# Second chunk's keys and state in 120 rows, state products per unit of eight heads

## The chip, the core and the metric

The kernel runs on one core of a Trainium2 chip. The core has a matrix engine (TensorE, PE in the profile, with its weight loads as PEld), a vector engine (VectorE, DVE), a scalar engine (ScalarE, ACT), GpSimd (POOL), and SyncE (SP), whose queue issues all of this kernel's transfers. They run side by side and wait for each other by semaphores. The metric is the time of the program on the device, in microseconds; lower is better. PE's clock is granted at 2.4 GHz (1.00 in the profile) or at half of it (0.50).

## What is computed

An mLSTM attention of 4 batches, 8 heads, 768 steps and 40 columns a head, and behind it two feed-forward layers over its 3072 rows of 320 columns, with 2048 hidden columns each:

```python
def _attn_ref(q, k, v, i_gate, f_gate, o_gate):
    ...
    for t in range(S):
        m_new = np.maximum(f_gate[:, :, t] + m, i_gate[:, :, t])
        f_stab = np.exp(f_gate[:, :, t] + m - m_new)
        i_stab = np.exp(i_gate[:, :, t] - m_new)
        ...
        C = f_stab[...] * C + i_stab[...] * np.einsum('bhd,bhe->bhde', vt, kt)
        n = f_stab[...] * n + i_stab[...] * kt
        h_tilde = np.einsum('bhde,bhe->bhd', C, qt)
        denom = np.maximum(np.abs(nq), 1.0)
        y[:, :, t] = o * h_tilde / denom

r = np.maximum(x @ w_in, 0.0);  x = (r * r) @ w_out
h = x @ w_in2;  x = np.where(h > 0, h, np.exp(np.minimum(h, 0)) - 1) @ w_out2
```

## The kernel before

**Tiling.** The steps are cut into 6 chunks of 128. A unit `u` is one chunk of one batch (24 units, 4 to a chunk), a half unit `n = 2u + g` is four of its heads. The state of a batch, 40 rows by 8 heads of 42 columns (values, the normalizer, a zero), is kept in `Cf[b]` across chunks.

**One half unit.** `mb_load` brings rows of running maxima, `mask` (POOL) and `emit_E` (ACT) make decay weights of them, `scores` (L283) multiplies keys and queries on PE into the bank `s`, `emit_P` (DVE, L289) joins both. `pv` (L302) then issues three kinds of products: `inter`, queries by state (`pv<-cf,rqk`, later `pv<-cst,qks`), `main`, weights by values (`pv<-kvo,mb`), and `st`, keys by values (`ut<-kvo`), which the state takes up. `evac` (DVE) joins the first two into `num` (L329, L333) and updates the state: a decay (L332) and an addition (L335). `norm`, `trans`, `x_hi` and `x_lo` finish a unit and lay it out as input of the first layer.

**Chunks differ.** The first chunk (`m_pe` to `evac0`) is written by hand and runs in the order of the code. In the second chunk (half units 8 to 15, below `NPLAIN`) queries, keys and state are plain 32-bit numbers in 40 rows (`qk_load`, `qk_hi`), and each product is two matmul instructions. From the third chunk on they are split in parts and stacked in 120 rows (`qk_stack`, `Cst`), with one instruction each. A form such as 40\*128 in the profile is the rows by the columns of the weights that an instruction uses.

**What sets the order.** Attention for the tile of 512 rows that comes next is woven into the feed-forward steps of the first layer. Steps of attention (`attn_pre`, `attn_pe`, `attn_post`, two to a half unit) are dealt out over the 16 hidden blocks of a tile; `emit_pe` puts their matmuls between the large ones `h<-xh,w` (first product) and `acc<-ghi,w` (second). During the first tile the weights are brought in as well (`raw<-wq`), and DVE and ACT convert them (`ct`, `cu`, `w`). Up to attention step 16 the order of PE, ACT, DVE and POOL is that of the code; behind it a scheduler sets the order of every engine at build time, and SP's throughout. PSUM banks `s`, `pv` and `ut` exist once each; `ut` also serves the transposes.

Of the kernel before, what the change touches and what calls it, by code (L numbers as in the profile page):

```python
# [6 lines left out]
F32 = mybir.dt.float32  # L7
# [34 lines left out]
def body(tc, qk, kvo, gates, wq, ident_in, qkm_in, out):  # L42
# [102 lines left out]
    Cf = [gc.tile([D, H * VW], F32, name=f"cf{b}") for b in range(B)]  # L145
# [80 lines left out]
    def qk_load(n):  # L226
        if n < N0:
            t = wp.tile([128, 2 * WC], F32, tag="w", name="rqk")[0:3 * D, 0:8 * L].rearrange("p (two t) -> p two t", two=2)
        else:
            t = a2.tile([3 * D, 2, 4 * L], F32, tag="qks" if n < NPLAIN and n % 2 else "rqk", name="rqk")  # L230
        k_ = D if n < NPLAIN else 3 * D
        sp.dma_start(out=t[0:k_], in_=qk[n, 0:k_])
        raw_t[n] = t

    def qk_hi(n):
        if n < NPLAIN:
            t = raw_t.pop(n)
            qS[n], kS[n] = t[0:D, 0], t[0:D, 1]
            return
        st = a2.tile([3 * D, 2, 4 * L], F32R, tag="qks", name="qks")  # L240
        act.activation(out=st, in_=raw_t[n], func=AF.Copy)
        qS[n], kS[n] = st[:, 0], st[:, 1]
# [48 lines left out]
    def pv(n):  # L291
        u, g = divmod(n, 2)
        c, b = divmod(u, B)
        p = mb_t.pop(n)
        q_ = qS.pop(n)
        t = kvo_t[u]
        ps = bank(n, "pv")
        PV_t[n] = ps
        inter, main, st = [], [], []

        def mm(to, o, l_, r_):
            to.append(lambda: pe.matmul(o, lhsT=l_, rhs=r_, start=True, stop=True))  # L302
# [12 lines left out]
        return inter, main, st

    def evac(n):
# [7 lines left out]
        cf3 = Cf[b][:, 4 * g * VW:4 * (g + 1) * VW].rearrange("p (h d) -> p h d", h=4)  # L325
        if keyed(u):
            u3 = U_t.pop(n)[0:D, 0:4 * VW].rearrange("p (h d) -> p h d", h=4)
        gb = cols[c % 2][:, 64 + b * H + 4 * g:64 + b * H + 4 * g + 4].unsqueeze(2).to_broadcast([128, 4, VW])
        dve.tensor_tensor(out=nu, in0=p[:, 4 * VW:8 * VW].rearrange("p (h d) -> p h d", h=4), in1=gb, op=ALU.mult)  # L329
        if keyed(u):  # L330
            db = decb[c % 2][:, b * H + 4 * g:b * H + 4 * g + 4].unsqueeze(2).to_broadcast([D, 4, VW])
            dve.tensor_tensor(out=cf3, in0=cf3, in1=db, op=ALU.mult)  # L332
        dve.tensor_tensor(out=nu, in0=pm, in1=nu, op=ALU.add)  # L333
        if keyed(u):
            dve.tensor_tensor(out=cf3, in0=u3, in1=cf3, op=ALU.add)  # L335
# [293 lines left out]
    def evac0(n):  # L629
# [5 lines left out]
        act.activation(out=Cf[u][:, 4 * g * VW:4 * (g + 1) * VW], in_=ps[0:D, 4 * VW:8 * VW], func=AF.Copy)  # L635
# [14 lines left out]
    pool_.affine_select(out=negmask, in_=mz, pattern=[[0, 4], [1, L]], compare_op=ALU.is_ge, fill=NEG, base=0, channel_multiplier=-1)  # L650
    early = es.enter_context(ExitStack())
# [134 lines left out]
def _layout(inputs):  # L786
# [12 lines left out]
    qk = np.concatenate([qk] * 3, axis=1)  # L799
    qkm = np.zeros((3 * D, 2), np.float32)  # L800
# [42 lines left out]
```

## Time and profile before

| | |
|---|---|
| three timed runs | 905.93, 900.64, 907.98 us (median 905.93) |
| profiled execution | 900.38 us, span 898.6 us, mean clock 0.978 |
| PE busy | 880.1 us, 98% |
| DVE busy | 556.1 us, 62% |
| ACT busy | 548.8 us, 61% |
| POOL busy | 140.3 us, 16% |
| transfers | 81.82 MB, mean 91 GB/s |

The profile is of one execution on the chip. Busy shares are means over stages with different limits, so the rows below are mostly of short stretches. Matmuls are pipelined, so an instruction's length overlaps the next one's; what a group of matmuls takes is read from its start to the start of the next group.

### The profile page before, as it was taken

The numbers are of one execution on the slowest core, as the hardware profiler recorded it, in microseconds if no ns is written. First come the engines' busy times: TensorE is split into PE (matmuls) and PEld (weight loads), VectorE is DVE, ScalarE is ACT, GpSimd is POOL, SyncE is SP. The second block draws the span as 40 slices with busy tenths as digits, with TensorE's granted clock in tenths as the row PEclk, the third lists the DMA queues.
The fourth block names the chain that finished last, engine by engine and source line by source line (L and its number), as shares of the span: only waits on it lengthen the run. The fifth ranks groups of instructions, "written<-read, shape, count | busy, mean of one in ns | idle before, by whom it ended". The sixth has DMA issues, their size and how long they took to land.

```text
span 898.6 us, 13340 instructions
## 1 busy us (share of the span) xinstructions
PE 880.1 (98%) x4813; PEld 744.0 (83%) x4818; DVE 556.1 (62%) x1027; ACT 548.8 (61%) x1045; POOL 140.3 (16%) x203
## 2 busy tenths in 40 slices
PE   9889999999999999999999998999999999999997
PEld 5768778778888887888888887898989999899996
DVE  2668978755555554454543699766566656655654
ACT  3549867555666566666746799555464555554543
POOL 1142013221211111110000000211112111111111
PEclk9867999999999999999999999999999999999999
DMA  8525453753343445334204354001020020000000
GB/s 248 194 96 162 163 177 116 208 99 83 111 131 95 105 121 151 100 102 142 80 25 158 108 196 144 1 28 50 1 77 1 1 77 1 22 9 1 30 1 30
DMA packets 31875, 81.82 MB, mean 91 GB/s; under 512 B 4578, under 2 KB 9666, under 8 KB 31810
## 3 DMA queue, kind: packets, MB, share of 16 engines
q1 hardware_dynamic: 31809, 80.98, 30.3%
q8 instruction: 38, 0.62, 0.3%
q14 instruction: 28, 0.22, 0.1%
HBM read 70.51 MB, written 8.73 MB: 88 GB/s over the span
## 4 chain that ended last, share of the span: by engine, by line
PE 85%; DMA 6%; DVE 4%; ACT 3%; issue 1%; POOL 0%; SPq 0%; POOLq 0%; DVEq 0%; ACTq 0%
PE h L485 38%; PE acc L526 36%; PE pv L302 5%; PE s L283 2%; DMA mb<-negm_dr 2%; PE ut L302 1%; DMA kvo<-kvo 1%; DMA rqk<-qk 1%; PE ut L376 1%; DMA yr<-y_dr 1%; PE pv L622 1%; DVE w L137 1%; DMA dec_dr<-gaw 1%; ACT mb L275 0%; DMA decb<-dec_dr 0%
## 5 line engine op out<-in xcount | busy, mean ns | idle before, releaser
L485 PE MATMUL h<-xh,w 128*128 128x512 f32 x1152 | 369.1, 405 | 3.2 <-DVE r L507 3.0
L485 PEld LDWEIGHTS h<-xh,w 128*128 128x128 f32 x1152 | 219.0, 191 | 48.4 <-DVE r L507 3.8
L509 DVE TENSOR_TENSOR glo<-r,ghi 128x512 fp32r<-128x512 f32 x192 | 132.2, 689 | 155.7 <-ACT r L499 85.1
L485 PE MATMUL h<-xl,w 128*128 128x512 f32 x384 | 155.0, 404 | 1.4 <-DVE xl L393 1.3
L526 PE MATMUL acc<-w,ghi 128*128 128x320 f32 x768 | 153.6, 309 | 0.6 <-POOL ghi L508 0.6
L503 ACT ACTIVATE r<-h 128x512 f32<-128x512 f32 x96 | 57.4, 598 | 144.1 <-PE h L485 98.5
L526 PE MATMUL acc<-ghi,w 128*128 128x512 f32 x480 | 139.8, 403 | 0.0
L526 PEld LDWEIGHTS acc<-w,ghi 128*128 128x128 f32 x768 | 126.0, 188 | 6.6 <-POOL ghi L508 1.1
L508 POOL TENSOR_SCALAR ghi<-r 128x512 fp32r<-128x512 f32 x96 | 61.3, 638 | 358.2 <-DVE r L507 137.9
L506 DVE SCALAR_TENSOR_TENSOR ex<-ex,th 128x512 f32<-128x512 f32 x96 | 68.5, 713 | 57.2 <-ACT ex L505 56.0
L526 PEld LDWEIGHTS acc<-ghi,w 128*128 128x128 f32 x480 | 88.0, 189 | 16.0
L526 PE MATMUL acc<-w,glo 128*128 128x320 f32 x384 | 99.2, 309 | 0.0
L275 ACT ACTIVATE mb<-mb,cols 128x128 f32<-128x128 f32 x160 | 51.4, 390 | 71.0 <-POOL mb L267 71.0
L526 PE MATMUL acc<-glo,w 128*128 128x512 f32 x288 | 89.8, 404 | 1.7 <-DVE glo L509 1.7
L485 PEld LDWEIGHTS h<-xl,w 128*128 128x128 f32 x384 | 73.8, 192 | 14.7 <-DVE xl L393 2.0
L497 ACT ACTIVATE r<-h 128x512 f32<-128x512 f32 x96 | 55.6, 585 | 35.1 <-PE h L485 31.7
L507 DVE SCALAR_TENSOR_TENSOR r<-h,ex 128x512 f32<-128x512 f32 x96 | 66.2, 690 | 2.8
L526 PEld LDWEIGHTS acc<-w,glo 128*128 128x128 f32 x384 | 67.4, 188 | 0.2
L498 ACT ACTIVATE ghi<-r 128x512 fp32r<-128x512 f32 x96 | 60.3, 628 | 10.2 <-PE acc L526 8.4
L267 POOL TENSOR_SCALAR_AFFINE_SELECT mb<-mb 128x512 f32<-128x512 f32 x40 | 33.1, 830 | 189.1 <-DMA mb<-negm_dr 138.1
L504 ACT ACTIVATE th<-r 128x512 f32<-128x512 f32 x96 | 60.7, 632 | 2.8
L526 PEld LDWEIGHTS acc<-glo,w 128*128 128x128 f32 x288 | 51.7, 188 | 11.8 <-DVE glo L509 2.3
(96 smaller groups left out, 1051.4 us busy)
## 6 DMA issues: line engine op xcount, KB each, us to landing
raw<-wq SPq DMA_DIRECT2D x32, 704.0 KB
rqk<-qk SPq DMA_DIRECT2D x32, 480.0 KB
kvo<-kvo SPq DMA_DIRECT2D x24, 488.0 KB
mb<-negm_dr SPq DMA_DIRECT2D x40, 256.0 KB
y_dr<-y SPq DMA_DIRECT2D x18, 256.0 KB
out<-y SPq DMA_DIRECT2D x24, 160.0 KB
yr<-y_dr SPq DMA_DIRECT2D x12, 256.0 KB
yr<-y_dr SPq DMA_DIRECT2D x24, 128.0 KB
```

Of the source, the lines that this page charges most:

```text
L275: act.activation(out=m[:, i, :], in_=m[:, i, :], func=AF.Exp, bias=cols[c % 2][:, col:col + 1])
L302: to.append(lambda: pe.matmul(o, lhsT=l_, rhs=r_, start=True, stop=True))
L485: lambda i=i, a=a, b_=b_: pe.matmul(h[:, 0:n], lhsT=a, rhs=b_, start=(i == 0), stop=(i == len(seq) - 1))
L497: act.activation(out=r, in_=h, func=AF.Relu)
L498: act.activation(out=hi, in_=r, func=AF.Square)
L503: act.activation(out=r, in_=h, func=AF.Relu, scale=-1.0)
L504: act.activation(out=th, in_=r, func=AF.Tanh, scale=0.5)
L506: dve.scalar_tensor_tensor(out=ex, in0=ex, scalar=1.0, in1=th, op0=ALU.add, op1=ALU.mult)
L507: dve.scalar_tensor_tensor(out=r, in0=h, scalar=0.0, in1=ex, op0=ALU.max, op1=ALU.subtract)
L508: pool_.tensor_scalar(out=hi, in0=r, scalar1=1.0, scalar2=1.0, op0=ALU.mult, op1=ALU.mult)
L509: dve.tensor_tensor(out=lo, in0=r, in1=hi.bitcast(F32), op=ALU.subtract)
L526: ops.append(lambda: pe.matmul(o, lhsT=l_, rhs=r_, start=first and st, stop=last and sp_))
```

## The change

- `qk_load` fetches 120 rows, not 40, for half units 8 to 15. The host fills the query rows 40 to 119 with copies and the key rows 40 to 119 with zeros.
- `Cf` has 120 rows, which four POOL memsets clear at the start; only rows 0 to 39 are written later. The products of the second chunk then run over 120 rows, and what the added rows contribute is zero.
- `pv` issues no state products for the first half of a unit (`g` = 0) and those of all 8 heads with the second, into one bank. `evac` decays and updates the state of all 8 heads at once, behind the second half; the two operations on `num` now stand before the state's.

```diff
-    Cf = [gc.tile([D, H * VW], F32, name=f"cf{b}") for b in range(B)]
+    Cf = [gc.tile([3 * D, H * VW], F32, name=f"cf{b}") for b in range(B)]
...
-        k_ = D if n < NPLAIN else 3 * D
+        k_ = D if n < N0 else 3 * D
         sp.dma_start(out=t[0:k_], in_=qk[n, 0:k_])
...
-            qS[n], kS[n] = t[0:D, 0], t[0:D, 1]
+            qS[n], kS[n] = t[:, 0], t[:, 1]
...
-        if keyed(u):
-            ut = bank(n, "ut")
-            U_t[n] = ut
         for i in range(4):
...
             mm(main, ps[:, o], p[:, i, :], v1)
-            if keyed(u):
-                mm(st, ut[0:D, o], t[:, h * D:(h + 1) * D], v1)
+        if keyed(u) and g:
+            U_t[u] = bank(n, "ut")
+            for h in range(H):
+                mm(st, U_t[u][0:D, h * VW:(h + 1) * VW], t[:, h * D:(h + 1) * D], t[:, DM + h * VW:DM + (h + 1) * VW])
...
-        if keyed(u):
-            db = decb[c % 2][:, b * H + 4 * g:b * H + 4 * g + 4].unsqueeze(2).to_broadcast([D, 4, VW])
+        dve.tensor_tensor(out=nu, in0=pm, in1=nu, op=ALU.add)
+        if keyed(u) and g:
+            cf3 = Cf[b][0:D].rearrange("p (h d) -> p h d", h=H)
+            u3 = U_t.pop(u)[0:D, 0:H * VW].rearrange("p (h d) -> p h d", h=H)
+            db = decb[c % 2][:, b * H:b * H + H].unsqueeze(2).to_broadcast([D, H, VW])
             dve.tensor_tensor(out=cf3, in0=cf3, in1=db, op=ALU.mult)
-        dve.tensor_tensor(out=nu, in0=pm, in1=nu, op=ALU.add)
-        if keyed(u):
             dve.tensor_tensor(out=cf3, in0=u3, in1=cf3, op=ALU.add)
...
+    for x in Cf:
+        pool_.memset(x, 0.0)
...
+    qk[:NPLAIN, D:, 1] = 0.0
```

The scheduler makes a new order from the first changed instruction on. On PE, where the second chunk begins, the order before is as follows (`ut<-kvo` state products, `s` scores, `pv<-cf` queries by state, `pv<-kvo,mb` weights by values, `h` feed-forward; a row with x4 is four products):

```order
L302 MATMUL ut<-kvo 40x42 x4
L283 MATMUL s<-rqk 128x128 x4
L302 MATMUL pv<-kvo,mb 128x42 x4
L302 MATMUL ut<-kvo 40x42 x4
L283 MATMUL s<-rqk 128x128 x4
L302 MATMUL pv<-cf_126,rqk 128x42 x4
L302 MATMUL pv<-kvo,mb 128x42 x4
L283 MATMUL s<-rqk 128x128 x4
L485 MATMUL h<-xh,w 128x512
```

And in the changed kernel, at the same place on PE:

```order
L302 MATMUL ut<-kvo 40x42 x8
L283 MATMUL s<-rqk 128x128 x4
L302 MATMUL pv<-kvo,mb 128x42 x4
L283 MATMUL s<-rqk 128x128 x4
L482 MATMUL h<-xh,w 128x512
L482 MATMUL h<-xl,w 128x512
L482 MATMUL h<-xh,w 128x512 x2
L482 MATMUL h<-xl,w 128x512
L482 MATMUL h<-xh,w 128x512 x3
L302 MATMUL pv<-cf_126,rqk 128x42 x4
L302 MATMUL pv<-kvo,mb 128x42 x4
```

The second group of state products has moved up to the first, and eight large matmuls now stand between the scores and the queries by state.

On DVE, from the second chunk's first decay on (`cf` the state, `num` the numerator, `mb` the joined scores, `ct` and `w` the conversion of a weight tile), before:

```order
L332 TENSOR_TENSOR cf_126<-cf_126,decb_121 40x168
L289 TENSOR_TENSOR mb<-s,mb 128x512
L335 TENSOR_TENSOR cf_126<-ut,cf_126 40x168
L289 TENSOR_TENSOR mb<-s,mb 128x512
L329 TENSOR_TENSOR num<-pv,cols_119 128x168
L333 TENSOR_TENSOR num<-pv,num 128x168
L137 TENSOR_TENSOR w<-ct,w 128x64
L137 TENSOR_TENSOR w<-ct,w 128x640
L289 TENSOR_TENSOR mb<-s,mb 128x512
L332 TENSOR_TENSOR cf_126<-cf_126,decb_121 40x168
L119 TENSOR_SCALAR ct<-ct 128x704
L335 TENSOR_TENSOR cf_126<-ut,cf_126 40x168
```

In the changed kernel, on DVE at that place:

```order
L289 TENSOR_TENSOR mb<-s,mb 128x512 x2
L325 TENSOR_TENSOR num<-pv,cols_119 128x168
L326 TENSOR_TENSOR num<-pv,num 128x168
L289 TENSOR_TENSOR mb<-s,mb 128x512
L137 TENSOR_TENSOR w<-ct,w 128x64
L137 TENSOR_TENSOR w<-ct,w 128x640
L119 TENSOR_SCALAR ct<-ct 128x704
L331 TENSOR_TENSOR cf_126<-cf_126,decb_121 40x336
L120 SCALAR_TENSOR_TENSOR ct<-raw,ct 128x704
L332 TENSOR_TENSOR cf_126<-ut,cf_126 40x336
```

The four state operations of the unit have become two of twice the columns, behind the third score product.

On SP, where the third chunk's gates are stored (`negm_dr`, `dec_dr`) and fetched again (`mb` mask rows, `decb` decays), with weight loads `raw`, before:

```order
L96 DMA raw<-wq 128x704
L180 DMA negm_dr<-gnm 32x128
L184 DMA dec_dr<-gaw 32x1
L356 DMA cst_123<-cst_123 40x336
L357 DMA cst_123<-clo 40x336
L223 DMA mb<-negm_dr 128x512
L187 DMA decb_120<-dec_dr 40x32
```

And in the changed kernel, on SP:

```order
L96 DMA raw<-wq 128x704
L180 DMA negm_dr<-gnm 32x128
L232 DMA rqk<-qk 120x1024
L184 DMA dec_dr<-gaw 32x1
L96 DMA raw<-wq 128x704
L223 DMA mb<-negm_dr 128x512 x2
L187 DMA decb_120<-dec_dr 40x32
```

A weight load has moved in between the store of the decays and the mask rows, and the state's two transfers `cst` have moved ahead of this place.

## Rows read from the trace of the kernel before

**Rows 1.** The page: busy time, share of the span, instructions; the clock in 40 slices

```profile
PE 880.1 (98%) x4813; PEld 744.0 (83%) x4818; DVE 556.1 (62%) x1027; ACT 548.8 (61%) x1045; POOL 140.3 (16%) x203
...
PEclk9867999999999999999999999999999999999999
```

**Rows 2.** Windows: length, busy us (instructions) of PE, PEld, DVE, ACT, POOL; PEclk, DMA share, GB/s

```profile
62.97:69.79 6.82, 5.48 (x14) 4.20 (x14) 6.28 (x10) 5.72 (x17) 4.39 (x5) 0.50 0.58 195
...
73.20:76.62 3.42, 3.42 (x32) 3.27 (x30) 3.29 (x10) 3.42 (x10) 0.25 (x1) 1.00 0.40 92
76.62:83.45 6.83, 6.83 (x26) 5.10 (x26) 6.79 (x14) 6.83 (x16) 3.15 (x4) 0.50 0.50 168
...
114.17:117.58 3.41, 3.41 (x22) 2.67 (x23) 3.25 (x8) 1.78 (x3) 0.00 (x0) 1.00 0.03 10
117.58:120.99 3.41, 3.41 (x11) 2.73 (x11) 0.62 (x2) 0.00 (x0) 0.44 (x1) 0.50 0.43 152
...
165.37:168.78 3.41, 2.94 (x29) 2.49 (x28) 2.79 (x8) 2.83 (x8) 1.44 (x2) 1.00 0.83 234
...
175.61:895.80 720.19, 712.54 (x3893) 616.41 (x3891) 429.91 (x753) 439.09 (x815) 102.20 (x161) 1.00 0.25 72
```

**Rows 3.** Timeline of PE, second chunk: start, length, line, operands, form, instructions

```profile
71.85 1.09 PE L302 MATMUL pv<-kvo,mb 128*128 128x42 f32 x8
72.87 0.50 PE L302 MATMUL ut<-kvo 128*40 128x42 f32 x8
...
74.30 0.98 PE L302 MATMUL pv<-cf,rqk 40*128 40x42 f32 x8
75.21 1.09 PE L302 MATMUL pv<-kvo,mb 128*128 128x42 f32 x8
76.22 1.74 PE L283 MATMUL s<-rqk 40*128 40x128 f32 x8
...
115.77 1.08 PE L302 MATMUL pv<-cf,rqk 40*128 40x42 f32 x8
116.78 1.23 PE L302 MATMUL pv<-kvo,mb 128*128 128x42 f32 x8
```

**Rows 4.** Timeline of PE, third chunk

```profile
166.90 1.07 PE L302 MATMUL pv<-kvo,mb 128*128 128x42 f32 x8
167.79 0.52 PE L376 MATMUL ut<-ident,xt 128*128 128x128 f32 x3
```

**Rows 5.** Windows: VectorE alone, from 63 to 118 us

```profile
63.00:118.00 55.00, 48.96 (x96) 0.87 0.46 152
```

**Rows 6.** Groups of VectorE by form: instructions, busy us, mean ns, idle before them

```profile
L367 DVE TENSOR_TENSOR num<-num,den 128x320 f32<-128x320 f32 x24 | 13.4, 559 | 0.6
...
L332 DVE TENSOR_TENSOR cf<-cf,decb 40x168 f32<-40x168 f32 x32 | 10.3, 354 | 28.5 <-DMA decb<-dec_dr 14.4 <-POOL clo L350 12.7 <-PE pv L302 1.3
L335 DVE TENSOR_TENSOR cf<-ut,cf 40x168 f32<-40x168 f32 x32 | 10.2, 319 | 2.5 <-PE ut L302 2.4
```

**Rows 7.** Windows of the start, columns as in rows 2

```profile
4.00:26.00 22.00, 21.68 (x140) 14.58 (x139) 6.57 (x20) 8.27 (x26) 1.40 (x2) 1.00 0.95 290
...
32.00:38.00 6.00, 5.84 (x48) 4.79 (x48) 5.32 (x12) 5.15 (x14) 1.85 (x2) 1.00 0.12 25
```

**Rows 8.** Timeline of POOL at the start

```profile
1.19 0.52 POOL L649 MEMSET mz<- 128x512 f32 x1
...
11.28 1.40 POOL L263 TENSOR_TENSOR kvo<-kvo,cols 128x320 f32<-128x320 f32 x2 [8.85 <-DVE cols L196]
```

**Rows 9.** Groups of weight loads by form, columns as in rows 6

```profile
L302 PEld LDWEIGHTS pv<-kvo,mb 128*128 128x128 f32 x320 | 47.5, 191 | 4.2
...
L302 PEld LDWEIGHTS pv<-cf,rqk 40*128 40x128 f32 x64 | 8.1, 187 | 3.3 <-issue 2.5 <-PE acc L526 0.7
```

**Rows 10.** Waits of the DMA queue up to 130 us: us in total, times, longest

```profile
SPq L96 <- DVE ct L120: 37.5, 10, 7.3
```

**Rows 11.** Timeline of VectorE where the third chunk's decay begins

```profile
121.52 1.30 DVE L332 TENSOR_TENSOR cf<-cf,decb 40x168 f32<-40x168 f32 x5 [3.32 <-DMA decb<-dec_dr]
```

More of the change, by code (lines that the diff above doesn't have):

```diff
@@ L324, in evac @@
         pm = p[:, 0:4 * VW].rearrange("p (h d) -> p h d", h=4)
-        cf3 = Cf[b][:, 4 * g * VW:4 * (g + 1) * VW].rearrange("p (h d) -> p h d", h=4)
-        if keyed(u):
-            u3 = U_t.pop(n)[0:D, 0:4 * VW].rearrange("p (h d) -> p h d", h=4)
         gb = cols[c % 2][:, 64 + b * H + 4 * g:64 + b * H + 4 * g + 4].unsqueeze(2).to_broadcast([128, 4, VW])
         dve.tensor_tensor(out=nu, in0=p[:, 4 * VW:8 * VW].rearrange("p (h d) -> p h d", h=4), in1=gb, op=ALU.mult)
-        if keyed(u):
-            db = decb[c % 2][:, b * H + 4 * g:b * H + 4 * g + 4].unsqueeze(2).to_broadcast([D, 4, VW])
+        dve.tensor_tensor(out=nu, in0=pm, in1=nu, op=ALU.add)
[3 more added lines that the diff above has]
+            db = decb[c % 2][:, b * H:b * H + H].unsqueeze(2).to_broadcast([D, H, VW])
             dve.tensor_tensor(out=cf3, in0=cf3, in1=db, op=ALU.mult)
-        dve.tensor_tensor(out=nu, in0=pm, in1=nu, op=ALU.add)
-        if keyed(u):
             dve.tensor_tensor(out=cf3, in0=u3, in1=cf3, op=ALU.add)
@@ L343, in c_hi @@
             b = u % B
-            act.activation(out=Cst[b][0:D], in_=Cf[b], func=AF.Copy)
+            act.activation(out=Cst[b][0:D], in_=Cf[b][0:D], func=AF.Copy)
     def c_lo(u):
@@ L349, in c_lo @@
             clo = a1.tile([D, H * VW], F32R, tag="clo", name="clo")
-            pool_.tensor_tensor(out=clo, in0=Cf[b], in1=Cst[b][0:D].bitcast(F32), op=ALU.subtract)
+            pool_.tensor_tensor(out=clo, in0=Cf[b][0:D], in1=Cst[b][0:D].bitcast(F32), op=ALU.subtract)
             clo_t[u] = clo
@@ L634, in evac0 @@
         dve.tensor_copy(num_t[u][:, 4 * g:4 * g + 4, :], ps[:, 0:4 * VW].rearrange("p (h d) -> p h d", h=4))
-        act.activation(out=Cf[u][:, 4 * g * VW:4 * (g + 1) * VW], in_=ps[0:D, 4 * VW:8 * VW], func=AF.Copy)
+        act.activation(out=Cf[u][0:D, 4 * g * VW:4 * (g + 1) * VW], in_=ps[0:D, 4 * VW:8 * VW], func=AF.Copy)
     dr = gc.tile([128, TT], BF16, name="dr")
```

## Prediction

> **What bounds the kernel now.** I read the page first: TensorE (PE) is busy for 98% of the span, and the clock row shows dips in the first quarter only [rows 1]. So the time is the sum of PE's own work, at the clock it is granted, and what shortens that work is worth its full length as long as no other engine steps in.
>
> Next I cut the early part into stretches where the clock stands still [rows 2]. The second chunk, the one the change touches, runs from about 60 us on. In it PE stands at 0.50 (1.2 GHz) three times: 62.97 to 69.79, 76.62 to 83.45 and 117.58 to 120.99, 17.06 us in all. Before the second fall there is no gap at all: PE is busy 3.42 of 3.42 us, with key-query products `s<-rqk` and state products `pv<-cf,rqk` in the form 40\*128, beside `pv<-kvo,mb` [rows 2, 3]. Before the third it is busy 3.41 of 3.41 us, again with `pv<-cf,rqk` and `pv<-kvo,mb` [rows 2, 3]. A stretch of like small matmuls in the third chunk, where the operands have 120 rows (165.37 to 168.78), ran at 1.00 and was not followed by a fall at once, though PE was busy for only 2.94 of 3.41 us [rows 2, 4].
>
> Third, I looked at what it costs PE to go from one array shape to another. The eight instructions `pv<-kvo,mb` take 0.89 us to the start of the next group where that group has the full 128\*128 shape (166.90 to 167.79, [rows 4]), and 1.02 and 1.01 us where the next is 128\*40 or 40\*128 (71.85 to 72.87, 75.21 to 76.22, [rows 3]). One change of shape costs about 0.12 us.
>
> Last, VectorE (DVE) in this stage: from 63 to 118 us it works 48.96 of 55.00 us [rows 5]. It converts the weights here, so it is nearly a second bound.
>
> **The change, part by part.** *40 rows become 120.* The matmuls stay as many and stream as many columns. Eight `pv<-cf,rqk` of 40 rows take 1.01 us to the next group, with a change of shape at the end (115.77 to 116.78); eight of 128 rows take 0.89 without one [rows 3, 4]. Less the 0.12 they are alike, so more rows cost nothing. What goes is the change of shape around them. Through the whole order of PE after the hand-ordered start, I count 139 changes of shape before and 69 after. About 52 of the 70 that go lie in the second chunk's stage: all those into and out of the 40-row form, and a few of the state product's. At 0.12 each that is 6.2 us; if only the way out is paid for, since a small group in the full shape may also wait on its way in, 3.1.
>
> *The state product per unit.* Two groups of eight 128\*40 instructions become one of sixteen, where the scheduler leaves them together. Of the 70 changes, about 18 fall into chunks three to five: 18 x 0.12 = 2.2 us, bounds 1.1 and 2.2. PE is alone in its way there (712.54 busy of 720.19 us, [rows 2]), so I take it in full.
>
> *The clock.* If the second chunk's stretches look to the clock like the third chunk's, the three dips go. Their price is half of PE's busy time in them: (5.48 + 6.83 + 3.41)/2 = 7.9 us [rows 2]. The lower bound is zero.
>
> *What DVE lets through.* So PE could give back up to 6.2 + 7.9 = 14.1 us between 60 and 121 us. DVE has 55.00 - 48.96 = 6.0 us free there [rows 5], and its order is fixed, so PE's products wait for it once that is used up. Its own work shrinks: per unit two decays of 354 ns and two additions of 319 ns become one each over 336 columns [rows 6]. No row has 40x336. The bounds are the 168-column time and twice that; nearest is the 128x320 multiplication at 559 ns, which holds some slow ones, so I take 530 ns. A unit then saves 2 x (354 + 319) - 2 x 530 = 286 ns, the four units of this stage 1.1 us. The stage can thus shrink by about 7.1 us. Not every idle gap of DVE closes, because its waits are for particular products; I take three quarters, 5.5 us. Bounds: 1.1 (DVE's own saving alone) and 7.1.
>
> *Loads.* Eight query-key loads grow from 160 to 480 KB, 2.6 MB in all. At 290 GB/s [rows 7] each takes 1.1 us longer. Four are issued in the first 26 us, where the DMA engines are at 0.95; the 4.4 us they add run into the quiet stretch from 32 to 38 us (share 0.12, [rows 7]), and nothing due before it is queued behind them but the second chunk's gates, mask rows and keys, which are used from 60 us on. The other four come singly between 62 and 105 us. Cost zero; without this cover 1.1 us each.
>
> *Clearing the state.* Four POOL memsets of 120x336, no more than 0.52 us each by the 128x512 one, at most 2.1 us. POOL is idle for 8.85 us before it is next wanted at 11.28 [rows 8], and the mask's first reader on PE stands behind the same gate columns. Cost zero; 2.1 us if POOL were waited for.
>
> Here a rule speaks against the change. The loads of weights take 187 ns in the 40\*128 form and 191 ns in the full one [rows 9], and both kinds of group advance by 0.11 us per matmul [rows 3, 4], so loads lie under other matmuls in either form. The Trainium skill (TensorE: Matmul & The Clock Gate, Part 3, "The mechanism") says that a weight load overlaps matmuls in flight only when the row group differs. With 120 rows all row groups are taken, so by that rule loads would no longer be hidden; by the rows they are hidden already in the full shape. By the rows nothing is added; the rule's sum is the third rival below.
>
> **Sum.** 5.5 + 2.2 = 7.7 us off the profiled run's 900.4 (a span of 898.6 and 1.8 us around it): 892.7. The profiled run sits at the low end: the timed runs are 900.6, 905.9 and 908.0, a median 5.5 us above it. One trace cannot show what the higher two did. Falls of the clock that come without any gap are the likeliest thing to differ from run to run, and the change removes these; I carry 2 us of the 5.5. Forecast: 894.5 us.
>
> **Rivals.** (a) *The added rows are zeros and earn no clock.* For it: nothing in this trace separates rows addressed from rows that hold data. Against it: first-chunk work aside, the dips follow the 40-row form. Then the dips stay, the shape changes give about the mean of 3.1 and 6.2, 4.6, plus 2.2, within DVE's room; the spread of the runs stays too: 905.9 - 6.8 = 899.1.
>
> (b) *DVE is the bound of the stage.* For it: 89% busy while it is also held up by PE. Then the stage gives DVE's own 1.1 and the late part 2.2: 900.4 - 3.3 = 897.1, and with half of the runs' spread 900.
>
> (c) *Weight loads come into the open.* 128 matmul instructions of the second chunk at 0.19 us each add 24.3 us to the forecast: 919. It decides from 0.16 us per matmul on: 128 x 0.16 = 20.5 us take 894.5 to 915. Against it stand the equal group times above.
>
> (d) *The SyncE queue.* In the new order a weight load `raw` stands ahead of two mask loads and of `decb`. Such a load has stood up to 7.3 us for DVE [rows 10], and DVE's decay of the state already waited 3.32 us for `decb` [rows 11], and a score product stands behind that decay in both orders. If the raw load waits 7.3 us there, mask rows and `decb` come that much later, PE starves for it, and a half-clock stretch like the third (3.41 us busy, 1.7 lost, [rows 2]) follows: 9.0 - 7.7 = +1.3, 907. It makes the kernel slower by over 1% only from a hold of about 15 us. For it: the order. Against: it is one load, and the 37.5 us that ten such loads stood before are 3.8 us each in the mean.
>
> **How the numbers follow.** Forecast (891 to 897) 0.50; (a) 0.20; (b) 0.16; (c) 0.02; (d) 0.08, of which 0.03 for a long hold; and 0.04 for a larger gain than DVE's room suggests, about 886. What a measurement of this kernel tells from no change is about 1%, so under 896.9 counts as faster and over 915.0 as slower. Forecast and larger gain make 0.54; a little of the forecast lies above 896.9 and a little of (a) below, which cancel. Slower: 0.02 + 0.03 = 0.05. Same: 0.41. The range 885 to 906 leaves out (c) and most of (d), and the far tail below. The forecast's own range is 889 to 898.
>
> **What would show it.** Right: granted clock 1.00 between 62 and 121 us but for stretches behind a real gap; `pv<-cf,rqk` and `s<-rqk` as 120\*128, eight `pv<-kvo,mb` in 0.89 us everywhere; DVE's state updates near 530 ns, its idle time from 63 to 118 us below 3 us; span near 891. Wrong: dips behind 120-row stretches without a gap (a); PE idle on `glo`, `xl` or `mb` of DVE in that stage (b); a group's spacing above 0.11 us at full clock (c); PE idle behind mask loads with SyncE standing on `ct` (d).

## Result: 898.55 us, 0.8% under the kernel before

The changed kernel takes 898.55 us (median of 8 runs, 893.61 to 899.45); the kernel before, timed beside it, 905.32 us (8 runs, 899.85 to 907.98). The ratio is 0.9917 with a 95% interval of 0.9893 to 0.9942: a gain clear of noise, but less than the 1% below which I had counted a time as "same" (over 896.9 us). I had given "faster" 0.54 and "same" 0.41. The value lies inside the range 885 to 906, 4.05 us above the forecast of 894.5 and 0.6 above the forecast's own range of 889 to 898. Ratios, here and further down, leave out runs over 1.5% above their kernel's fastest (five of e7's twelve, one each of e8's and e11's six); medians and ranges leave out none.

The profiled run of the changed kernel took 898.73 us (span 896.9). Its page, the lines that answer to [rows 1]:

```profile
PE 873.7 (97%) x4818; PEld 744.5 (83%) x4818; DVE 554.8 (62%) x995; ACT 549.0 (61%) x1045; POOL 138.7 (15%) x207
...
PEclk9669998999999999999999999999999999999999
```

TensorE works 6.4 us less, and its low clock has moved: it now stands at the very start of the row. The windows of the same trace, cut where the clock changes (columns as in [rows 2]):

```profile
30.59:61.31 30.72, 30.05 (x142) 24.20 (x143) 14.84 (x34) 10.90 (x29) 3.55 (x4) 0.50 0.50 159
61.31:136.41 75.10, 68.63 (x418) 55.95 (x416) 64.33 (x129) 61.24 (x122) 16.96 (x18) 1.00 0.54 173
136.41:143.23 6.82, 6.82 (x20) 5.76 (x21) 6.27 (x13) 5.46 (x9) 2.56 (x2) 0.50 0.90 250
143.23:894.16 750.93, 739.48 (x4072) 640.57 (x4070) 457.92 (x789) 460.19 (x854) 109.11 (x168) 1.00 0.26 76
```

Three things stand here. The three falls of [rows 2] between 62 and 121 us are gone: 1.00 from 61.31 to 136.41. A new one stands at 136.41. And the first chunk, whose products are unchanged, lost its clock for 30.72 us in this run, where the profiled run of before lost it for 17.07 (39.07 to 56.14). So the two profiled runs differ by only 1.65 us, and their ends must not be compared: TensorE's first product of the first layer (`h<-xh,w`) starts at 67.39 us, before at 62.37. I therefore measure from that first `h` product to the 513th (`h<-xh,w` and `h<-xl,w` counted together), which lies behind the last state product, the last thing that the change touches: 351.5 us before, 344.2 after.

What the change was to do to the shapes and to the state's update is there. TensorE in the second chunk, against [rows 3]:

```profile
85.49 0.98 PE L302 MATMUL pv<-cf,rqk 120*128 120x42 f32 x8
86.30 1.06 PE L302 MATMUL pv<-kvo,mb 128*128 128x42 f32 x8
87.19 1.14 PE L283 MATMUL s<-rqk 120*128 120x128 f32 x8
```

Eight `pv<-kvo,mb` now advance to the next group in 0.89 us (86.30 to 87.19), as in the third chunk [rows 4], and eight `pv<-cf,rqk` in 0.81 where they took 0.91 and 1.01. VectorE's groups, against [rows 6]:

```profile
L331 DVE TENSOR_TENSOR cf<-cf,decb 40x336 f32<-40x336 f32 x16 | 9.0, 570 | 30.2 <-POOL clo L347 15.3 <-DMA decb<-dec_dr 14.3 <-PE pv L302 0.6
L332 DVE TENSOR_TENSOR cf<-ut,cf 40x336 f32<-40x336 f32 x16 | 7.9, 492 | 1.2 <-PE ut L302 1.2
```

570 + 492 = 1,062 ns a unit, where I had put 2 x 530.

The new loss is the next three views, all of the changed kernel. SyncE's queue (start, length):

```profile
113.61 0.42 SPq L180 DMA_DIRECT2D negm_dr<-gnm  x1
114.26 0.34 SPq L232 DMA_DIRECT2D rqk<-qk  x1
114.88 0.31 SPq L184 DMA_DIRECT2D dec_dr<-gaw  x1
116.30 0.35 SPq L96 DMA_DIRECT2D raw<-wq  x1
119.94 0.82 SPq L223 DMA_DIRECT2D mb<-negm_dr  x2
122.69 0.29 SPq L187 DMA_DIRECT2D decb<-dec_dr  x1
```

VectorE, which [rows 11] showed at 3.32 us:

```profile
121.72 0.68 DVE L506 TENSOR_TENSOR glo<-r,ghi 128x512 fp32r<-128x512 f32 x1
127.22 0.93 DVE L331 TENSOR_TENSOR cf<-cf,decb 40x336 f32<-40x336 f32 x2 [4.82 <-DMA decb<-dec_dr]
```

TensorE, 9 us later, right before the half clock:

```profile
134.60 0.42 PE L302 MATMUL pv<-cf,rqk 120*128 120x42 f32 x2
136.34 1.62 PE L523 MATMUL acc<-glo,w 128*128 128x512 f32 x3 [1.33 <-DVE glo L506]
```

Counted from each kernel's first `pv<-cf` (61.46 us before, 66.58 after), the changed kernel was 12.8 us ahead at the seventh half unit's (140.84 and 133.17 us); at the eighth's (152.84 and 150.55) 7.4 were left.

### The profile page after: what moved, and what is told of

It is laid out like the page before. It is cut to its first block, busy times and chain, and to the rows that moved or that the text cites. A ratio compares the mean times of both kernels' runs of the same rounds, so it can differ in the third digit from the quotient of the medians.

```text
span 896.9 us, 13320 instructions
## 1 busy us (share of the span) xinstructions
PE 873.7 (97%) x4818; PEld 744.5 (83%) x4818; DVE 554.8 (62%) x995; ACT 549.0 (61%) x1045; POOL 138.7 (15%) x207
## 4 chain that ended last, share of the span: by engine, by line
PE 80%; DVE 6%; DMA 6%; ACT 3%; issue 2%; POOL 1%; SPq 0%; POOLq 0%; DVEq 0%; ACTq 0%
PE h L482 35%; PE acc L523 34%; PE pv L302 4%; DMA mb<-negm_dr 3%; PE dps L641 2%; PE s L283 1%; ACT mb L275 1%; PE pv L619 1%; PE ut L302 1%; PE ut L373 1%; DVE ct L120 1%; DMA dec_dr<-gaw 1%; DMA raw<-wq 1%; DVE w L137 1%; DMA yr<-y_dr 1%
## 5 line engine op out<-in xcount | busy, mean ns | idle before, releaser
L482 PEld LDWEIGHTS h<-xh,w 128*128 128x128 f32 x1152 | 215.9, 189 | 46.7 <-DVE r L504 3.7
L482 PE MATMUL h<-xl,w 128*128 128x512 f32 x384 | 152.1, 396 | 1.7 <-DVE xl L390 1.7
L523 PE MATMUL acc<-glo,w 128*128 128x512 f32 x288 | 92.5, 409 | 5.1 <-DVE glo L506 5.1
L267 POOL TENSOR_SCALAR_AFFINE_SELECT mb<-mb 128x512 f32<-128x512 f32 x40 | 30.2, 757 | 225.4 <-DMA mb<-negm_dr 146.8
```

The source lines that it names most:

```text
L482: lambda i=i, a=a, b_=b_: pe.matmul(h[:, 0:n], lhsT=a, rhs=b_, start=(i == 0), stop=(i == len(seq) - 1))
L523: ops.append(lambda: pe.matmul(o, lhsT=l_, rhs=r_, start=first and st, stop=last and sp_))
```

## The experiments

My theory: the rows earn shape and clock as forecast, and VectorE's wait for `decb` takes part of it back. Rivals: the clock goes by data; the unit of 8 earns it; VectorE caps the stage. The runs, each against the kernel before on its own chip ("h to h" is the first to the 513th `h` product of its profiled run; "half clock" the stretches that begin between 62 and 160 us there):

| run | rows | heads | decay | median us | ratio to before (95%) | h to h | half clock |
|---|---|---|---|---|---|---|---|
| before | 40 | 4 | memory | 905.3 | 1 | 351.5 | 17.1 |
| changed | 120 | 8 | memory | 898.6 | 0.9917 (0.9893 to 0.9942) | 344.2 | 6.8 |
| e1 | 120, zeros in both | 8 | memory | 898.5 | 0.9934 (0.9914 to 0.9954) | 347.9 | 6.8 |
| e2 | 120 | 4 | memory | 915.4 | 1.0113 (1.0088 to 1.0138) | 361.0 | 17.1 |
| e3 | 40 | 8 | memory | 905.6 | 1.0016 (0.9997 to 1.0036) | 349.6 | 10.2 |
| e4 | 120 | 8 | memory, GpSimd | 904.8 | 1.0009 (0.9981 to 1.0037) | 348.2 | 6.8 |
| e5 | 120 | 8 | TensorE | 893.5 | 0.9890 (0.9857 to 0.9922) | 338.7 | 3.4 |
| e6 | 120 | 4 | TensorE | 894.3 | 0.9905 (0.9875 to 0.9936) | 340.7 | 3.4 |
| e7 | 40 | 4 | TensorE | 906.4 | 0.9984 (0.9950 to 1.0018) | 349.4 | 10.2 |
| e8 | changed, fillers | 8 | memory | 895.0 | 0.9895 (0.9860 to 0.9930) | 346.0 | 13.7 |
| e9 | 40 | 8 | TensorE | 903.7 | 0.9996 (0.9965 to 1.0026) | 347.1 | 17.1 |
| e10 | 120 in scores only | 8 | TensorE | 894.3 | 0.9896 (0.9867 to 0.9924) | 339.5 | 0 |
| e11 | 120, fillers | 8 | TensorE | 887.7 | 0.9810 (0.9775 to 0.9845) | 342.6 | 3.4 |
| e12 | 120 | 8 | memory, in place | 894.8 | 0.9891 (0.9858 to 0.9924) | 339.5 | 3.4 |

The last two columns are of one run each: e1's profiled run was the slowest of its eleven, e9's the quickest of its twelve. And a kernel whose first `h` comes earlier has a longer "h to h" for that alone (e11 against e5: 8.0 us earlier, 3.9 longer), so part of the 7.3 us between the kernel before and the changed one, whose first `h` is 5.0 us later, may be the later start.

**e1: is it the rows or the data?**

```diff
-    qk[:NPLAIN, D:, 1] = 0.0
+    qk[:NPLAIN, D:] = 0.0
```

> The program of the changed kernel, instruction for instruction; only the input data differ: rows 40 to 119 of the second chunk's queries are zeros too, where the changed kernel has real queries moving over zero keys. The result is computed in full. Theory (the rows that an instruction addresses count for the clock, whatever stands in them): granted clock 1.00 from 62 to 130 us with no stretch of 0.50, and the time of the changed kernel, 893.6 to 899.5 us. Rival (the clock follows the data that toggle in the array, so that the real queries in the added rows earned it): the 0.50 stretches at 63, 76 and 117 us come back as in the kernel before, 17 us of them or 8.5 us lost, and the time goes to 901 to 908 us.

The time is that of the changed kernel. The profiled run has two stretches of half clock of 3.41 us each in the second chunk, at 69.21 and 137.47 us, behind waits of TensorE of 1.61 us (for `xl`) and 1.69 us (for `glo`); between them:

```profile
72.62:137.47 64.85, 61.47 (x383) 51.64 (x381) 55.84 (x113) 54.98 (x107) 10.13 (x10) 1.00 0.59 186
```

The falls of before do not come back. "No stretch of 0.50" was too strict, but zeros on both sides hold the clock as well as real queries over zeros: of the two theories, the rows that the instruction addresses count.

**e2 and e3: each half alone.** e2 is the changed kernel with `pv` and `evac` of before, of which the core:

```diff
-        if keyed(u) and g:
-            U_t[u] = bank(n, "ut")
-            for h in range(H):
-                mm(st, U_t[u][0:D, h * VW:(h + 1) * VW], t[:, h * D:(h + 1) * D], t[:, DM + h * VW:DM + (h + 1) * VW])
+            if keyed(u):
+                mm(st, ut[0:D, o], t[:, h * D:(h + 1) * D], v1)
```

e3 is the changed kernel with the 40 rows of before:

```diff
-        k_ = D if n < N0 else 3 * D
+        k_ = D if n < NPLAIN else 3 * D
...
-            qS[n], kS[n] = t[:, 0], t[:, 1]
+            qS[n], kS[n] = t[0:D, 0], t[0:D, 1]
```

> Only the first half of the change: second chunk's queries, keys and state in 120 rows, the state's products and update per half of 4 heads as before. The order has 101 changes of tile shape behind the hand-ordered start, against 139 before and 69 in the changed kernel. Theory (shape and clock both pay, and add): no half clock from 62 to 110 us, and the second chunk gains 38 changes x 0.12 = 4.6 us and the 7.9 us of half clock, so interval of states 4 to 7 is 8 to 12.5 us shorter than before, and the whole 3 to 4 us longer than the changed kernel: 897 to 903 us. Rival (VectorE is the cap in that stage, 6 us of room as predicted): with its 14 more updates VectorE holds the stage to a gain of 6 us at the most.

> Only the second half of the change: products and update of the state per unit of 8 heads; queries, keys and state of the second chunk stay in 40 rows. 96 changes of shape behind the start, against 139 before. Theory (the 120 rows are what holds the clock): the stretches of 0.50 between 63 and 120 us stay, about 15 to 20 us of them, and 43 changes x 0.12 = 5.2 us are gained, of that 3 in the second chunk: 899 to 903 us. Rival (the clock fell because of the gaps and small products that the unit of 8 removes): no half clock there, and the second chunk gains as much as in the changed kernel, 12.8 us.

Neither theory had e2 at 915.4 us, 10 us slower than before. Its stage was as fast as the changed kernel's up to 120 us. Then VectorE, TensorE and SyncE of e2, one after the other:

```profile
119.46 0.88 DVE L120 SCALAR_TENSOR_TENSOR ct<-raw,ct 128x704 int32<-128x704 int32 x1
130.91 1.06 DVE L332 TENSOR_TENSOR cf<-cf,decb 40x168 f32<-40x168 f32 x4 [10.57 <-DMA decb<-dec_dr]
```

```profile
131.12 1.65 PE L526 MATMUL acc<-ghi,w 128*128 128x512 f32 x3 [7.31 <-ACT ghi L498]
```

```profile
122.00 1.82 SPq L187 DMA_DIRECT2D decb<-dec_dr  x1
```

The decays of 32 numbers, 5 KB when broadcast, were issued at 122.00 and VectorE went on at 130.91; TensorE starved 7.31 us, and 10.24 us of half clock began in that standstill. This is the changed kernel's loss in large. e3 shows the other half: 905.6 us, as before and above its theory's 899 to 903. Its half clock, 10.24 us, is less than the 15 to 20 expected, and comes behind a gap of 0.97 us for `mb`:

```profile
65.50:79.15 13.65, 11.88 (x83) 9.20 (x81) 11.27 (x19) 10.01 (x27) 7.59 (x8) 1.00 0.37 119
79.15:89.39 10.24, 9.77 (x36) 8.34 (x35) 9.83 (x21) 10.11 (x25) 2.13 (x3) 0.50 0.50 152
```

**e4: is it SyncE's queue?**

```diff
-        sp.dma_start(out=dec_dr[c].unsqueeze(1), in_=aw[0:32, 2, L - 1:L])
+        pool_.dma_start(out=dec_dr[c].unsqueeze(1), in_=aw[0:32, 2, L - 1:L])
-        sp.dma_start(out=decb[c % 2], in_=dec_dr[c].partition_broadcast(D))
+        pool_.dma_start(out=decb[c % 2], in_=dec_dr[c].partition_broadcast(D))
```

> The changed kernel with the two small transfers of the decay (dec to memory, and its broadcast back) issued from GpSimd's queue instead of SyncE's; TensorE's and VectorE's orders are the same row for row. Theory (the raw and mask loads ahead of the broadcast on SyncE's queue made VectorE wait 4.82 us at 127 us, that starved TensorE at 136 us, and the half clock of 6.8 us behind it cost 3.4): the wait at 127 us is under 1.5 us, no half clock near 136 us, third chunk's first units 5 us earlier than in the changed kernel, and the whole 3 to 5 us shorter: 889 to 895 us. Rival (the broadcast is not what is late, or its landing is not the queue's doing): the same stretch at 136 us and the time of the changed kernel, 893.6 to 899.5 us.

Worse, 904.8 us, above the range of either side: the theory falls. GpSimd's own issues carry landing times in the trace (issue view: queue, count, KB, us to landing):

```profile
dec_dr<-gaw POOLq DMA_DIRECT2D x1, 0.1 KB, 8.1
decb<-dec_dr POOLq DMA_DIRECT2D x1, 5.0 KB, 5.4
```

and VectorE and TensorE of that run:

```profile
129.17 0.92 DVE L331 TENSOR_TENSOR cf<-cf,decb 40x336 f32<-40x336 f32 x2 [8.01 <-DMA decb<-dec_dr]
```

```profile
131.18 2.08 PE L283 MATMUL s<-rqk 120*128 120x128 f32 x8 [3.22 <-DVE mb L289]
```

Nothing stood ahead of 128 bytes on that queue, and they took 8.1 us, beside raw, key and mask loads in flight (the changed kernel's DMA engines are at 0.98 from 116 to 120 us). On SyncE's queue it is much the same: in the changed kernel `decb`, issued as soon as `dec_dr` had landed, went out 7.8 us behind it (114.88 to 122.69), and VectorE went on 4.5 us later (127.22). The transfer is slow, not its issue. The Trainium skill (DMA: Bandwidth & Descriptors, "Anatomy of one DMA — SWDGE (gpsimd) path") gives a fixed part of about 2.0 us per transfer, and its "Rules for kernel authors" say that other issuing engines bring no bandwidth, as all share the same 16 DMA engines. The second agrees with e4, where another queue did not shorten the wait (8.01 us against 4.82); the first is far from 8.1 us under this load.

**e5, e6, e7: the decay without the road through memory.** One more small matmul broadcasts the decays in the bank that the gate columns use anyway, and `gate_dec` and `gate_decb` go; e5 has this on the changed kernel, e6 on e2, e7 on the kernel before:

```diff
+        ops.append(lambda: pe.matmul(ps[:, 96:128], lhsT=aw[0:32, 2, L - 1:L].to_broadcast([32, 128]), rhs=ident[0:32, 0:32], start=True, stop=True))
-        dve.tensor_copy(cols[c % 2], G_ps.pop(c)[:, 0:96])
+        dve.tensor_copy(cols[c % 2], G_ps.pop(c)[:, 0:128])
-            db = decb[c % 2][:, b * H:b * H + H].unsqueeze(2).to_broadcast([D, H, VW])
+            db = cols[c % 2][0:D, 96 + b * H:96 + b * H + H].unsqueeze(2).to_broadcast([D, H, VW])
```

> The changed kernel without the decay's round trip through memory: one more matmul of 32 rows behind the three transposes of the gate values broadcasts the 32 decays to all partitions, the copy behind it takes 128 columns instead of 96, and the updates read that tile; the two small transfers per chunk are gone. Theory (the small transfers land late behind bulk loads: the 128 bytes issued at 115.34 us in the run with GpSimd's queue landed at 123.44, the 5 KB behind them at 129.08; VectorE stood 8.01 us): no wait on a transfer at the first update of the third chunk, no half clock behind it, 3.4 us of half clock and 1.3 us of starving gone, 889 to 895 us. Rival (the masks come over the same road and are late next, so that TensorE waits for VectorE's masked scores instead): a wait of 1.5 us or more there and 895 to 900 us.

> Only the 120 rows (products and update of the state per half, as before), and the decay by TensorE. Theory (what made the rows alone slower than before, 915 us, was VectorE's wait of 10.57 us for the decay at 120 to 131 us and what it starved): 897 to 903 us, some 3 to 5 us above the changed kernel with decay by TensorE (32 more changes of shape x 0.12 = 3.8 us). Rival (the updates per half cost VectorE that much themselves, or the loss behind 170 us has another cause): 908 us or more.

> The kernel before with the decay by TensorE. Theory: its wait for the decay was 3.32 us and starved TensorE by nothing (no wait of TensorE over 0.5 us between 110 and 160 us), so there is 0 to 3 us to gain, 902 to 905 us, and the change measured without the round trip (this kernel against the changed one with decay by TensorE) gains 8 to 13 us. Rival (the round trip costs both alike): this one gains as much as the changed kernel does.

e6 settles e2: 915.4 becomes 894.3 us (ratio 1.0113 to 0.9905), a little better than expected. With the road through memory the whole excess is gone. e5 is as expected, 893.5 us; in its trace VectorE goes through the same place without a stop:

```profile
119.88 0.88 DVE L119 SCALAR_TENSOR_TENSOR ct<-raw,ct 128x704 int32<-128x704 int32 x1
120.67 0.91 DVE L325 TENSOR_TENSOR cf<-cf,cols 40x336 f32<-40x336 f32 x2
```

From the changed kernel to e5 the intervals of the whole times overlap; h to h (344.2 to 338.7 us) and the missing wait carry this, not the medians. e7 gains nothing in its time, 906.4 us where 902 to 905 were expected: before, the wait was harmless.

**e9: the rows by themselves.** e3 with the diff of e5. Its order of matmuls is that of e5, one for one, and VectorE's is too.

> Products and update per unit of 8 heads and the decay by TensorE, with queries, keys and state of the second chunk in 40 rows: its order of matmuls, of VectorE's work and of the queues is that of the changed kernel with decay by TensorE (893.5 us), so the two differ by the 120 rows alone, 101 changes of shape against 67. Theory (rows give shape and clock): half clock of 10 to 17 us between 62 and 120 us against 3.4 there, so 3.4 to 6.8 us, and 34 x 0.12 = 4.1 us of shape: 901 to 905 us. Rival (with the decay's wait gone the 40 rows do as well): 893 to 897 us.

903.7 us, as the theory said. At the same place of the order, TensorE of e5 and then of e9:

```profile
93.80 0.85 PE L474 MATMUL h<-xh,w 128*128 128x512 f32 x3
94.49 1.06 PE L277 MATMUL s<-rqk 120*128 120x128 f32 x8
95.38 0.98 PE L296 MATMUL pv<-cf,rqk 120*128 120x42 f32 x8
96.19 0.94 PE L515 MATMUL acc<-glo,w 128*128 128x512 f32 x3
96.97 0.98 PE L296 MATMUL pv<-kvo,mb 128*128 128x42 f32 x8
```

```profile
91.54 0.86 PE L474 MATMUL h<-xh,w 128*128 128x512 f32 x3
92.33 1.16 PE L277 MATMUL s<-rqk 40*128 40x128 f32 x8
93.33 0.98 PE L296 MATMUL pv<-cf,rqk 40*128 40x42 f32 x8
94.24 0.97 PE L515 MATMUL acc<-glo,w 128*128 128x512 f32 x3
95.04 0.98 PE L296 MATMUL pv<-kvo,mb 128*128 128x42 f32 x8
```

The way into the 40-row form costs 0.79 - 0.69 = 0.10 us ahead of the scores and 1.00 - 0.89 = 0.11 within them (the second product starts 0.21 us behind the first, each later one 0.11 behind the last); the way out costs 0.91 - 0.81 = 0.10. To the `pv<-kvo,mb` behind it the visit takes 3.50 us against 3.17: 0.33 for two changes of shape. The sixteen visits that both traces make at full clock and without a gap cost 0.33 us in the mean, so 0.16 a change. And e9 has three falls of the clock; the last two have no gap of TensorE over 0.15 us shortly ahead:

```profile
63.23:70.06 6.83, 5.51 (x14) 4.15 (x14) 6.11 (x9) 5.72 (x17) 4.45 (x5) 0.50 0.52 185
87.13:90.54 3.41, 3.41 (x10) 2.63 (x9) 3.41 (x8) 3.23 (x6) 0.00 (x0) 0.50 0.78 261
124.67:131.50 6.83, 6.83 (x20) 5.72 (x21) 4.68 (x11) 6.50 (x13) 0.00 (x0) 0.50 0.27 97
```

Worked out as in the prediction, the rows are worth 34 x 0.12 = 4.1 us and (5.51 + 3.41 + 6.83)/2 less 1.7 for e5's one fall, 6.2 us; together 10.3. At 0.16 a change they are 5.4 + 6.2 = 11.6. The medians differ by 10.2, h to h by 8.4. The clocks of the timed runs agree with the two traces: their mean granted clock is 0.957 to 0.976 in e9's twelve runs and 0.970 to 0.985 in e5's six.

**e10: which of the rows?**

```diff
-            mm(inter, ps[:, (4 + i) * VW:(5 + i) * VW], q_[:, i * L:(i + 1) * L], (Cf if n < NPLAIN else Cst)[b][:, h * VW:(h + 1) * VW])
+            r_ = slice(0, D if n < NPLAIN else 3 * D)
+            mm(inter, ps[:, (4 + i) * VW:(5 + i) * VW], q_[r_, i * L:(i + 1) * L], (Cf if n < NPLAIN else Cst)[b][r_, h * VW:(h + 1) * VW])
```

> The changed kernel with decay by TensorE, where only the scores' products use 120 rows; the products of query and state in the second chunk go over the first 40 rows. 86 changes of shape against 67 and 101. Theory A (shape counts, by its changes): 19 x 0.12 = 2.3 us over 893.5, with the clock held by the scores (4 products of 128 columns against 4 of 42 in each half): 895 to 897 us. Theory B (any stretch of 40 rows costs the clock): half clock of 10 us or more between 62 and 120 us as with 40 rows in both, 900 to 905 us.

```profile
60.51:162.91 102.40, 98.47 (x581) 79.60 (x579) 89.96 (x178) 84.09 (x163) 27.68 (x26) 1.00 0.57 175
```

Theory A: no half clock in the whole chunk, and 894.3 us, just under its 895 to 897. (The next fall, at 162.91 us, comes behind a standstill of 1.56 us.) The 2.3 us for its 19 more changes of shape are not to be seen; h to h they are 0.8, and the times do not resolve them. The scores' rows alone hold the clock.

**e12: is it the transfer, or where VectorE waits for it?** In the order of the changed kernel, as in that of before, VectorE decays the state for the third chunk (`decb` of that chunk) in the middle of the second, as soon as the sources allow; the addition that needs it comes at 172.68 us in the changed kernel, 45 us behind the wait. e12 binds the decay to its place in the code:

```diff
-        dve.tensor_tensor(out=nu, in0=pm, in1=nu, op=ALU.add)
+        tc.keep_in_program_order(dve.tensor_tensor(out=nu, in0=pm, in1=nu, op=ALU.add))
-            dve.tensor_tensor(out=cf3, in0=cf3, in1=db, op=ALU.mult)
+            tc.keep_in_program_order(dve.tensor_tensor(out=cf3, in0=cf3, in1=db, op=ALU.mult))
```

> The changed kernel with the decays' road through memory left as it is, but VectorE's updates of the numerator and its decays of the state bound to the order of the code, so that the third chunk's decays stand behind that chunk's first numerators and no longer in the middle of the second chunk. Theory (nothing needs the third chunk's decay at 127 us; VectorE stands for it only because its order has it there): no wait of VectorE on the broadcast, no half clock near 136 us, 889 to 895 us, as with the decay by TensorE. Rival (the small transfers' slowness is that of all transfers there, and masks and loads hold the stage just as long): a wait of 3 us or more on masks or loads at the same place, 896 to 900 us.

```profile
L331 DVE TENSOR_TENSOR cf<-cf,decb 40x336 f32<-40x336 f32 x16 | 8.2, 510 | 0.0
```

All 16 decays ran with no idle time ahead of them (30.2 us in the changed kernel, 14.3 of it for `decb`), though the decays still travel through memory; 894.8 us, and 339.5 h to h, near e5's 338.7 (the interval of its whole time overlaps that of the changed kernel, as e5's does). e12's order is new as a whole, but its masks came no earlier: GpSimd went on with the two at 124.42 and 129.70 us, in the changed kernel with both at 126.73. So the cause was neither the queue nor the transfer as such, but an early place in an in-order engine's list for work that was not yet due.

The standstill at 136 us is the smaller part of what this cost the changed kernel. From the first `h` to the fourth chunk's first `pv<-cst` (235.69 us before; 233.54, 232.27 and 232.53 in the changed kernel, e5 and e12) these three gain 7.2, 8.4 and 8.1 us on the kernel before (e5 in spite of 6.83 us of half clock from 165.26 us on). From there to the 513th `h` the four take 178.2, 178.0, 173.8 and 174.2 us. So most of what e5 and e12 win back lies in the later chunks, where VectorE waits in early decays again. TensorE's waits (us in total, times, longest) from 210 to 300 and from 300 to 420 us in the changed kernel, then from 210 to 300 in e12 (e5 has none in either):

```profile
PE acc L523 <- ACT ghi L495: 1.4, 2, 1.2
PE acc L523 <- DVE glo L506: 0.6, 1, 0.6
...
PE acc L523 <- DVE glo L506: 1.4, 1, 1.4
PE acc L523 <- ACT ghi L495: 0.3, 1, 0.3
```

```profile
PE acc L523 <- ACT ghi L495: 0.5, 1, 0.5
```

One of the changed kernel's five, 0.58 us at 264.89, stands right behind a wait of VectorE for `decb` of 4.38 us, as does one of 1.87 us at 185.22, ahead of the stretch, behind a wait of 5.12. For the other four the trace shows no such wait, so how the early decays cost the rest of it stays open.

**e8 and e11: the first chunk.** Fillers are matmuls whose results are never read. e8 adds them to the changed kernel as shown; e11 adds them to e5, with 8 instead of 4 at the seventh and 16 at the ninth place.

```diff
-        idle((8, 6, 2, 2, 2, 2, 2, 2, 2, 4, 2)[i])
+        idle((8, 6, 4, 4, 4, 4, 4, 4, 4, 4, 2)[i])
```

> The changed kernel with 4 instead of 2 filler matmuls (their results are never read) in each of the first chunk's steps 2 to 8. Theory (the run-to-run spread of 5.5 us and TensorE's late start of the second chunk come from the half clock of 17 or 31 us that begins in the first chunk where TensorE stands 0.7 us for VectorE; two more fillers of 0.216 us stand in those gaps): clock 1.00 or a half-clock stretch no longer than 17 us before 60 us, first h at 57 to 63 us instead of 67.39, and 887 to 894 us in nearly all runs. Rival (the clock falls all the same, and 7 x 0.43 to 0.86 us of fillers are added): 899 to 904 us.

> The changed kernel with the decay by TensorE and with 4 fillers in the first chunk's steps 2 to 8, but 8 in step 6 and 16 in step 8, where TensorE stood 0.88 and 3.09 us for VectorE in the run with 4 everywhere. Theory (both losses are apart and add): no half clock before 60 us, first h at 57 to 61 us, no wait on a transfer at the third chunk's first update: 884 to 890 us, below the 893.5 and 895.0 us of either alone. Rival (what the start gains is waited away later, since VectorE and the loads have the same work to do by then): first h earlier, but the unit at 145 to 150 us no earlier, 891 to 895 us.

e8's 895.0 us lies between its two theories: in its trace the clock held until a wait of 3.09 us for VectorE. In e11 it held through the whole chunk:

```profile
24.00:51.34 27.34, 23.37 (x187) 17.89 (x184) 21.12 (x49) 13.55 (x38) 5.41 (x6) 1.00 0.77 214
51.34:58.17 6.83, 6.83 (x28) 4.33 (x29) 1.24 (x6) 2.06 (x4) 0.00 (x0) 0.50 0.29 93
```

```profile
30.00:58.00 28.00, 27.10 (x194) 18.59 (x193) 19.07 (x45) 14.31 (x36) 4.57 (x6) 1.00 0.56 181
```

e11 starts its first `h` at 59.28 us against 67.32 in e5, of which 4.2 us are left at the 513th: part is waited away, as its rival said. It takes 887.7 us, ratio 0.9810 (0.9775 to 0.9845), below both kernels and below e5; one of its six runs, outside the ratio, took 900.22.

## Why the prediction was right, and where it was not

**The clock: right.** Nine falls begin between 62 and 160 us in the profiled runs of the four kernels whose scores have 40 rows (before 3, e3 1, e7 2, e9 3), and seven of them have no gap of TensorE over 0.4 us shortly ahead. In the ten kernels whose scores have 120 rows there are fourteen falls, and each begins behind or within a standstill of 1.3 to 7.3 us. An earlier start is not what separates them: e8 and e11, with 120 rows, reach their first `h` at 62.22 and 59.28 us, as early as the kernel before, and have no fall without such a standstill. Rival (a) falls by e1.

**The price of a shape, 0.12 us: too small.** It is 0.16 where e5 and e9 can be laid side by side, because a group waits within itself as well on its way in; "less the 0.12 they are alike" compared a 40-row group that held this second wait with `pv<-kvo,mb`, while `pv<-cf,rqk` in 120 rows takes 0.81 us. The count was also split wrongly: in the orders of the two traces, 44 of the 70 changes that go lie ahead of 160 us and 26 behind, not 52 and 18.

**The late 2.2 us: not there in this kernel.** Behind the fourth chunk's first `pv<-cst` it gains 0.2 us. Where the decay does not travel through memory the term is there and larger: in that stretch 8 heads in place of 4 gain 3.2 us (e6 177.0, e5 173.8) and 5.3 (e7 178.8, e9 173.5). "PE is alone in its way there" is the step that failed: with the early decays bound to their place (e12) the stretch takes 3.8 us less. The ratios of whole times do not tell 8 heads from 4.

**DVE's room: mis-sized.** I capped a gain of 14.1 us at 7.1 and took 5.5; the chunk had gained 12.8 by 133 us, and kept 7.2 to the fourth chunk. The step that failed is "its order is fixed", with DVE's work of a stretch of the old kernel taken as what it must do in the new one. From the first `pv<-cf` to that of the fifth half unit, before and then after:

```profile
61.46:115.77 54.31, 52.97 (x267) 41.03 (x265) 48.27 (x94) 45.26 (x91) 12.09 (x13) 0.87 0.48 156
```

```profile
66.58:111.39 44.81, 40.47 (x250) 33.77 (x249) 40.23 (x78) 38.71 (x80) 10.86 (x13) 1.00 0.58 184
```

DVE is as full as it was (89% and 90%), its idle time from 63 to 118 us is 5.0 us where I had named less than 3 as a sign of being right, and TensorE stood 1.7 us for its `xl` there. So rival (b) had the right engine; but DVE does 8 us less there. The new order holds three weight conversions between the first and the fourth numerator of the chunk where the old one holds six, and makes them up later. That stood in the orders before anything ran. What its state updates would cost was right: 570 and 492 ns for two times 530.

**Weight loads, rival (c): wrong**, as the equal group times said: 64 loads of `pv<-cf,rqk` in the new form take 191 ns each, and eight such matmuls advance in 0.81 us. The rule of the Trainium skill (TensorE: Matmul & The Clock Gate, Part 3, "The mechanism") is not what this trace shows for full row groups. The same section also lets a load go ahead when it targets the background weight buffer, which the prediction left out; no run here shows whether that is what happens.

**Rival (d): the right place, the wrong cause.** VectorE's wait for `decb` grew from 3.32 to 4.82 us, TensorE starved, half a clock followed, as (d) had it with a chance of 0.08. But SyncE did not stand 7.3 us at `raw`; it waited 3.2 and 1.9 us for the landing of `negm_dr` and `dec_dr` beside bulk loads, and the place of the decay in VectorE's order made that count.

**The sum: right by cancelling.** 7.7 us were forecast; by the ratio 905.3 x (1 - 0.9917) = 7.5 came. In the two traces it is 7.2 to the fourth chunk, where 5.5 stood in the sum, and 0.2 behind it, where 2.2 stood. That these meet is luck.

**The base: wrong, and this is the 4 us.** The sum was made against a run 5.5 us under the median, and "I carry 2 us of the 5.5", because the second chunk's falls were to be what differs from run to run (892.7 + 2 is 894.7, not 894.5). They are gone, and the changed kernel's runs still spread over 5.8 us. 892.7 + 5.5 would have been 898.2.

The mean granted clock of the timed runs shows two groups in both kernels. Of the 73 runs of the kernel before that were timed beside the experiments, 20 took 898.0 to 902.0 us at a clock of 0.972 to 0.979, and 53 took 902.4 to 908.8 at 0.965 to 0.972. Of the changed kernel's eight, three took 893.6 to 895.0 us at 0.981 to 0.985, and five 898.4 to 899.5 at 0.975 to 0.978. The profiled run of before is of its lower group, that of after of its upper one, so their ends lie close; within a group the change takes 6 to 7 us off. The first chunk can hold the difference: its half clock took 17.1 us in the profiled run of before, 30.7 in that of after, 41.0 in e3's, and 0.007 of mean clock over 904 us are, by estimate, 13 us at half of it.

No trace shows a run of the other group of either kernel, and what makes the difference stays open: of one program there are only two traces, the changed kernel's and e1's, both with an early fall (30.59 and 28.25 us), and e11, whose profiled run keeps the clock there, has a run of 900.22 too. Whether the larger loads, which I put at zero, make an early fall likelier is open as well: all eight traced kernels with 120 rows and no more fillers have one (28.25 to 33.76 us), of the four with 40 rows only e3 (24.54), but each is one run.

## What to carry to other kernels

Where the clock falls behind many small matmuls of few rows, without a gap ahead, widen their operands to the full rows, with zeros if need be, and try one kind of product by itself: here the scores alone were enough. When an edit speeds up a stage, look in the new order for work that waits on a transfer and is not due yet: an in-order engine passes that wait on to everything behind it, and binding that work to its place was worth 4.7 us h to h here, beside the 7.3 of the edit itself. Take a forecast gain off the median, and take credit for a smaller spread only if more than one run has shown where the spread comes from.

## What was not expected of the hardware

128 bytes to memory took 8.1 us and 5 KB back 5.4 us beside bulk loads, from a queue of their own. Rows that hold only zeros, in weights and in moving data, held the clock like real ones (e1), and the scores' rows alone were enough (e10). TensorE's clock fell behind 40-row stretches in which the engine was busy without a gap (3.41 of 3.41 us ahead of two falls each of before and e9); in the ten kernels with 120 rows it fell between 62 and 160 us only behind or within a standstill of 1.3 us or more. Behind 160 us, where the scores of all kernels have 120 rows, three falls follow gaps of 0.49 us at most (before at 172.19, e2 at 180.99, e6 at 166.88), the others, but for the one at the end of each run, 1.5 us or more. A visit to the 40-row form cost 0.33 us, and part of it stood inside the group.
